# Joining the halves of the exponentials' sums with adding transfers in three pairs, and splitting the PSUM banks of the MLP into two pools

## The chip, the cores and the metric

One NeuronCore of a Trainium2 chip runs the whole program. The metric is the device time of one execution in microseconds. The page and the trace come from one profiled execution of the kernel before, with a span of 915.6 us. In the page PE is TensorE (PEld its weight loads), DVE is VectorE, ACT is ScalarE, POOL is GpSimd and SP is SyncE.

## The reference

Two blocks, one after the other. The first is attention with routing: batch B = 4, H = 8 heads, S = 768 positions, D = 64 columns per head. Queries and keys are each assigned to the nearest of 16 centroids, and a query only sees keys of its own cluster.

```python
mask = q_assign[:, :, :, None] == k_assign[:, :, None, :]
scores = scale * np.matmul(q, k.transpose(0, 1, 3, 2))
scores = np.where(mask, scores, -1000000000.0)
...
attn = np.exp(scores)
attn = attn / (np.sum(attn, axis=-1, keepdims=True) + 1e-09)
return np.matmul(attn, v).astype(np.float32)
```

The heads are laid side by side to rows of 512, and the second block is an MLP with 2048 hidden units and a residual:

```python
xn = (x - mu) / np.sqrt(var + 1e-06) * g_ln
ch = np.maximum(xn @ w_ch1, 0.0) @ w_ch2
return (x + ch).astype(np.float32)
```

All of it is computed in float32. The sum of the exponentials over the keys, the denominator of the softmax, is what the first part of the change touches.

## The kernel before

**Attention.** The work goes by pairs of heads: 16 pairs, numbered n = 0 to 15, four to a batch. A pair has two halves of 384 queries, g = 0 and g = 1; each half is one slot of the main loop. A slot has six steps, one for each block of 128 keys. In a step `scores` (L385) multiplies keys with queries for both heads of the pair and adds the mask by another product, and ScalarE takes the exponential of the result into a tile `e` (L380), with keys on the partitions and the queries of both heads side by side. Two steps share one tile of `e`, so a slot fills three tiles of 128 x 1536. `weigh` (L397) multiplies the values with `e`.

**The sums.** `add_up` (L415 to L438) adds the three tiles of a slot on VectorE into a tile `two`: first two of them (L432), then the third (L435). `two` still holds two halves of 768 columns, for the even and the odd steps. For pairs in `NARROW` (7, 8, 9, 10, 14) one more VectorE addition joins the halves (L437); for the others both stay. `sums` notes which halves there are.

**The denominator.** `finish(n, 0)` (L446 to L465) sums `two` over its 128 partitions by products with a matrix of ones into the PSUM tile `den_ps` (L451): four matmuls for a half, one for each head and each half of the queries, set beside one another on 32 columns of the array each. With both halves that is eight matmuls, with one joined half it is four. ScalarE copies the result to `dsb` (L460), and GpSimd's queue sends it by DRAM to `rdens` in another layout (`flat`, L462, and L463). `finish(n, 1)` takes the reciprocal (L467), sends it back to DRAM (`row`, L469) and loads it broadcast over the partitions (`rb`, two transfers, L477). `finish(n, 2)` and `finish(n, 3)` multiply the weighed values by it and store them.

**The order.** In the attention loop the instructions of TensorE, VectorE, ScalarE and GpSimd are in the order in which the program is written: nothing is moved by a scheduler there. SyncE's queue alone is left to it. In the first slot of pair n the order on TensorE is: the six scores, the denominator of pair n - 1, the centroid similarities of pair n + 1 (`sim_ps`, L304), the six weighings. In GpSimd's queue the first slot has `flat` and `rdens` of pair n - 1 and, at its end, a transfer that adds a converted part of the weights (`w<-tb`, L273, also an adding transfer, in `join_weight`). In the second slot it has `row` and `rb` of pair n - 1. The written order of the end of a slot matters for the change:

```python
            for i in own:
                weigh(i)
            add_up(n, slot, (0,))
            if slot and n and nxt:
                finish(n - 1, 1)
            if nxt:
                add_up(n, slot, (1,))
            if m:
                join_weight(m)
```

**PSUM.** PSUM has eight banks. In attention they are six for the scores, one for `a_ps` and `den_ps`, and one for the rest. After attention `stage.close()` gives them back, and one pool `ps_m` with eight banks is opened for all that follows.

**The MLP.** Per batch, each layer is computed in blocks with seven products for each eight of a plain block product. In both layers three kinds of PSUM tiles occur. `x_ps` and `z_ps` live long: a product is written, read out, and the next product is added into the same bank later. `y_ps` is written once and read once. Besides these, `stat_ps` (L564) and `flag_ps` (L762) are short transposes: the statistics of the rows of the next batch, and in batch 0 a check on the range of the denominators, which VectorE reads at L764. In the second layer (`second_layer`) each part runs over three row tiles `tt`, with eight matmuls (sixteen records) per product. From the second layer of batch 0 on only TensorE's order is as written; the other engines are ordered by the scheduler.

Of the kernel before, what the change touches and what calls it, by code (L numbers as in the profile page):

```python
# [13 lines left out]
ALU = mybir.AluOpType  # L14
AX = mybir.AxisListType
PSUM = bass.MemoryType.PSUM
# [3 lines left out]
def kernel(  # L20
# [11 lines left out]
    nc = tc.nc  # L32
# [3 lines left out]
    P = 128  # L36
# [19 lines left out]
    def pool(name, bufs, **kw):  # L56
        return stage.enter_context(tc.tile_pool(name=name, bufs=bufs, **kw))
# [10 lines left out]
    pools = {"t": pool("ps_t", 1, space=PSUM), "conv": conv}  # L68

    def ps(name, dt=F32, n=512):  # L70
        return pools["t"].tile([P, n], dt, tag="t", name=name)

    pairs = [(b, pr) for b in range(B) for pr in range(NPAIR)]
    loaded = {n: {} for n in range(len(pairs))}
# [1 line left out]
    TWICE = 7  # L76

    NARROW = (7, 8, 9, 10, 14)


    def load_blocks(n, name):
# [112 lines left out]
    def turn_centroids():  # L194
        ct_ps = ps("ct_ps")
        nc.tensor.transpose(ct_ps[:D, : H * NCL], c_sb, ident[: H * NCL, : H * NCL])
        ct_v = ct_ps[:D, : H * NCL].rearrange("p (r j c) -> p r j c", j=2, c=NCL)
        for j in range(2):
            nc.vector.tensor_copy(cT[j * D : (j + 1) * D, :, j, :], ct_v[:, :, j, :])
# [97 lines left out]
    def prep_sims(n):  # L297

        _, pr = pairs[n]
        sim = ps("sim_ps")  # L300
        for side in range(2):
            for g in range(NHALF):
                r = (g * 2 + side) * Q
                nc.tensor.matmul(  # L304
                    sim[r : r + Q, :HC],
                    cT[:, pr, :, :].rearrange("p j c -> p (j c)"),
                    prepared[n][side][:, g * HC : (g + 1) * HC],
                    start=True,
                    stop=True,
                    tile_position=(0, r),  # L310
                )
        prepared[n]["sim"] = sim
# [50 lines left out]
    sums = {}  # L363
# [51 lines left out]
    def add_up(n, g, parts=range(2)):  # L415
        u = (n * NHALF + g) * NT // 2
        if n + 1 == len(pairs):

            es = xpool.tile([P, 2, HC], F32, tag="row", name="es", bufs=2)
            e = [two[:, h] for two in [soft.pop(u + m) for m in range(NT // 2)] for h in range(2)]  # L420
            for m in range(1, NT):
                nc.vector.tensor_tensor(es, e[0] if m == 1 else es, e[m], ALU.add)
            sums[n, g] = [es]
            return
        if 0 in parts:
            if g == 0:
                two = xpool.tile([P, 3, S], F32, tag="sums", name="two", bufs=2)[:, :2]
            else:
                two = last.tile([P, 2, S], F32, tag="two", name="two", bufs=1)
            two = two.rearrange("p h (j c) -> p h j c", j=2)  # L430
            sums[n, g] = two
            nc.vector.tensor_tensor(two, soft.pop(u), soft.pop(u + 1), ALU.add)  # L432
        if 1 in parts:
            two = sums[n, g]
            nc.vector.tensor_tensor(two, two, soft.pop(u + 2), ALU.add)  # L435
            if n in NARROW:
                nc.vector.tensor_tensor(two[:, 0], two[:, 0], two[:, 1], ALU.add)  # L437
            sums[n, g] = [two[:, h] for h in range(1 if n in NARROW else 2)]  # L438

    def finish(n, part):
        b, pr = pairs[n]
        if part == 0:
            den = ps_a.tile([P, 512], F32, tag="a", name="den_ps") if n + 1 < len(pairs) else ps("den_ps")
            parts = len(sums[n, 0])  # L446
            for h in range(parts):
# [238 lines left out]
    with tc.manual_schedule(engines=order | {mybir.EngineType.Pool}):  # L686
        for u in range(len(pairs) * slots):
            n, slot = divmod(u, slots)
# [30 lines left out]
# [7 lines that stand above are left out]
# [42 lines left out]


    stage.close()  # L770
    pools["t"] = pool("ps_m", 8, space=PSUM)
    hid = pool("hid", 2)
    rest = ExitStack()
    pools["conv"] = rest.enter_context(tc.tile_pool(name="rest", bufs=1))
# [443 lines left out]
```

## Time and profile before

| | |
|---|---|
| time, median of 3 | 916.98 us (916.11 to 920.95) |
| span of the profiled execution | 915.6 us |
| attention, up to the last denominator | 0 to about 329.6 us |
| MLP | 329.7 us to the end |
| TensorE busy | 905.1 us |
| VectorE busy | 605.7 us, most of it in attention |
| DMA, mean over the span | 98 GB/s |
| granted TensorE clock | 0.999 |
| `den_ps` matmuls, two halves or one (L451) | 200 records, 19.2 us busy |
| last addition of `two` (L435) | 30, mean 1756 ns |
| joining addition on VectorE (L437) | 10, mean 958 ns |
| adding transfer `w<-tb`, 256 KB | 32, median 6.1 us to landing |

The page has a row for each group of instructions, with its busy time, the mean of one in ns, and the idle time of its engine just before it with what ended that. A float32 matmul leaves two records, so 200 records are 100 matmuls. A DMA row on GpSimd shows the time in which the transfer was issued; its time to landing is given apart. VectorE's load is uneven: in the slices of attention it is busy for seven to nine tenths, in the MLP for three to six.

### The profile page before, as it was taken

How to read it: one execution, taken by the hardware profiler on the slowest of the kernel's cores; microseconds unless marked ns; L12 is line 12 of the kernel's file. 1: busy time of each engine (PE TensorE's matmuls, PEld its weight loads, DVE VectorE, ACT ScalarE, POOL GpSimd, SP SyncE). 2: the span in 40 equal slices, each digit the busy share in tenths (PEclk: the TensorE clock that was granted, in tenths of full speed). 3: DMA queues.
4: the chain of work that ended last, by engine and by line, in shares of the span. 5: the costliest groups of instructions: out<-in, count | busy, mean ns of one | idle time of the engine just before them, and what ended most of it. 6: DMA issues, size and time to landing. Idle time of an engine off the chain costs nothing.

```text
span 915.6 us, 12228 instructions
## 1 busy us (share of the span) xinstructions
PE 905.1 (99%) x4556; PEld 576.9 (63%) x4556; DVE 605.7 (66%) x1060; ACT 365.7 (40%) x619; POOL 77.3 (8%) x141
## 2 busy tenths in 40 slices
PE   8999999999999999999999999999999999999997
PEld 5444444444444455578885568886558887557886
DVE  7999999899889878988843446542436372445330
ACT  4777777998877643330003330003331001332000
POOL 1122222111121112100000000000000000000000
PEclk9999999999999999999999999999999999999999
DMA  7888999997886346663520003120002120000011
GB/s 151 169 177 160 185 180 196 193 217 142 203 172 123 75 123 156 141 172 116 166 74 0 1 0 104 58 74 7 1 1 92 52 70 29 0 1 13 23 47 38
DMA packets 186579, 89.33 MB, mean 98 GB/s; under 512 B 153632, under 2 KB 170128, under 8 KB 186512
## 3 DMA queue, kind: packets, MB, share of 16 engines
q1 hardware_dynamic: 177200, 73.09, 33.6%
q0 software_dynamic: 7712, 14.99, 8.3%
q8 instruction: 38, 0.62, 0.3%
q10 hardware_dynamic: 1600, 0.39, 0.2%
q14 instruction: 29, 0.24, 0.1%
HBM read 62.52 MB, written 17.52 MB: 87 GB/s over the span
## 4 chain that ended last, share of the span: by engine, by line
PE 65%; ACT 0%; DVE 0%; issue 0%
PE x_ps L880 18%; PE x_ps L787 18%; PE z_ps L880 9%; PE z_ps L787 9%; PE y_ps L880 5%; PE y_ps L787 5%; PE s_ps L385 1%; PE a_ps L397 1%; PE den_ps L451 0%; ACT late L460 0%; DVE o_sb L903 0%; PE stat_ps L564 0%; PE flag_ps L762 0%
## 5 line engine op out<-in xcount | busy, mean ns | idle before, releaser
L380 ACT ACTIVATE e<-s_ps 128x768 f32<-128x768 f32 x192 | 151.7, 812 | 9.2 <-PE s_ps L385 4.6
L385 PE MATMUL s_ps<-t,t 64*128 64x384 f32 x768 | 154.9, 483 | 0.0
L397 PE MATMUL a_ps<-e,v_sb 128*64 128x384 f32 x768 | 130.9, 490 | 0.0
L397 PEld LDWEIGHTS a_ps<-e,v_sb 128*64 128x64 f32 x768 | 52.3, 137 | 75.8 <-issue 62.6
L807 DVE TENSOR_TENSOR h<-z_ps,u 128x384 f32<-128x384 f32 x64 | 35.6, 556 | 88.6 <-PE z_ps L787 67.4
L385 PEld LDWEIGHTS s_ps<-t,t 64*128 64x128 f32 x768 | 68.2, 188 | 35.1 <-issue 34.2
L880 PE MATMUL x_ps<-w2t,h 128*128 128x256 f32 x384 | 84.5, 379 | 0.0
L815 ACT ACTIVATE h<-h 128x384 f32<-128x384 f32 x96 | 49.5, 522 | 86.3 <-DVE h L807 86.3
L880 PEld LDWEIGHTS x_ps<-w2t,h 128*128 128x128 f32 x384 | 72.7, 190 | 10.1
L385 PE MATMUL s_ps<-mask,mask 64*128 64x384 bf16 x384 | 63.0, 324 | 1.1 <-ACT e L380 0.7
L432 DVE TENSOR_TENSOR two<-e 128x1536 f32<-128x1536 f32 x30 | 52.6, 1753 | 14.3 <-ACT e L380 14.0
L802 ACT COPY u<-x_ps 128x384 f32<-128x384 f32 x64 | 30.6, 479 | 75.9 <-PE x_ps L787 75.9
L802 ACT COPY p<-x_ps 128x384 f32<-128x384 f32 x32 | 14.9, 467 | 97.5 <-PE x_ps L787 97.5
L435 DVE TENSOR_TENSOR two<-two,e 128x1536 f32<-128x1536 f32 x30 | 52.7, 1756 | 1.7
L891 DVE TENSOR_TENSOR o_sb<-x_ps,xb 128x256 f32<-128x256 f32 x48 | 20.1, 418 | 49.4 <-PE x_ps L880 49.4
L787 PE MATMUL x_ps<-xn,w 128*128 128x384 f32 x128 | 46.6, 487 | 0.6 <-ACT late L460 0.6
L787 PE MATMUL x_ps<-xn,ws 128*128 128x384 f32 x128 | 46.5, 486 | 0.0
L787 PE MATMUL y_ps<-xn,w 128*128 128x384 f32 x128 | 46.5, 486 | 0.0
L787 PE MATMUL z_ps<-xt,ws 128*128 128x384 f32 x128 | 46.5, 486 | 0.0
L787 PE MATMUL x_ps<-xt,ws 128*128 128x384 f32 x128 | 46.5, 486 | 0.0
L787 PE MATMUL x_ps<-xt,w 128*128 128x384 f32 x128 | 46.5, 486 | 0.0
L787 PE MATMUL z_ps<-xn,ws 128*128 128x384 f32 x128 | 46.5, 486 | 0.0
(151 smaller groups left out, 1330.4 us busy)
## 6 DMA issues: line engine op xcount, KB each, us to landing
raw<-in_moe_w_ch_dram SPq DMA_DIRECT2D x32, 512.0 KB, 5.6
w<-tb POOLq DMA_DIRECT2D x32, 256.0 KB, 6.1
v_sb<-in_v_dram SPq DMA_DIRECT2D x32, 192.0 KB, 5.4
xr<-x_d SPq DMA_DIRECT2D x24, 256.0 KB, 3.1
xb<-x_d SPq DMA_DIRECT2D x48, 128.0 KB, 2.1
out_dram<-o_sb SPq DMA_DIRECT2D x48, 128.0 KB, 1.7
q_sb<-in_q_dram SPq DMA_DIRECT2D x62, 96.0 KB, 3.4
k_sb<-in_k_dram SPq DMA_DIRECT2D x62, 96.0 KB, 5.9
```

What stands on the lines that cost most here:

```text
L380: nc.scalar.activation(e, s[:, :, :HC], AF.Exp, scale=SCALE)
L385: nc.tensor.matmul(s[:, j, :HC], of_keys[:, keys], of_queries[:, o : o + HC], start=part == first, stop=part != first, skip_group_check=True,)
L397: nc.tensor.matmul(acc[j * D : (j + 1) * D, :HC], loaded[n]["v"][:, j, c, :], e[:, j, :], start=(c == 0), stop=(c == NT - 1),)
L432: nc.vector.tensor_tensor(two, soft.pop(u), soft.pop(u + 1), ALU.add)
L435: nc.vector.tensor_tensor(two, two, soft.pop(u + 2), ALU.add)
L787: nc.tensor.matmul(bank[:, :HC], lhs[:, c, :], rhs[:, c, :], start=first and c == 0, stop=c == NDH - 1, skip_group_check=True,)
L802: nc.scalar.copy(t, bank[:, :HC])
L807: nc.vector.tensor_tensor(h, bank[:, :HC], other, ALU.add)
L815: nc.scalar.activation(h, h, AF.Relu)
L880: nc.tensor.matmul(bank[:, :MH], hidden[lhs + (c,)][:, tt * P : (tt + 1) * P], rhs[:, c, :], start=first and c == 0, stop=c == NFH - 1, sk ...
L891: nc.vector.tensor_tensor(o, bank[:, :MH], x, ALU.add)
```

## The change

In the pairs 11, 12 and 13 (`CARRIED`) the two halves of `two` are joined as well, but not by VectorE: a transfer issued from GpSimd's queue reads the second half and adds it onto the first. With that `sums` has one half, and the denominator of these pairs needs four matmuls instead of eight. The transfer is issued in `add_up`, in each of the two slots of a pair, and moves 128 x 768 float32, 384 KB.

In the MLP the eight banks are split: `x_ps` and `z_ps` come from a pool of six, all others (`y_ps`, `stat_ps`, `flag_ps`) from a pool of two. It is meant to keep the short-lived tiles from taking turns with the long-lived ones.

```diff
     def ps(name, dt=F32, n=512):
-        return pools["t"].tile([P, n], dt, tag="t", name=name)
+        p = pools["long" if "long" in pools and name in ("x_ps", "z_ps") else "t"]
+        return p.tile([P, n], dt, tag="t", name=name)
...
     NARROW = (7, 8, 9, 10, 14)
+
+    CARRIED = (11, 12, 13)
...
             if n in NARROW:
                 nc.vector.tensor_tensor(two[:, 0], two[:, 0], two[:, 1], ALU.add)
-            sums[n, g] = [two[:, h] for h in range(1 if n in NARROW else 2)]
+            elif n in CARRIED:
+                nc.gpsimd.dma_start(out=two[:, 0], in_=two[:, 1], accum_op=ALU.add)
+            sums[n, g] = [two[:, h] for h in range(1 if n in NARROW + CARRIED else 2)]
...
     stage.close()
-    pools["t"] = pool("ps_m", 8, space=PSUM)
+
+    pools["long"], pools["t"] = pool("ps_m", 6, space=PSUM), pool("ps_n", 2, space=PSUM)
     hid = pool("hid", 2)
```

## Prediction

> **What bounds the kernel now.** I read the busy shares first, then the slices, then the chain of waits, then TensorE, GpSimd and VectorE in order of time around the denominators of pairs 11 to 13.
>
> ```profile
> PE 905.1 (99%) x4556; PEld 576.9 (63%) x4556; DVE 605.7 (66%) x1060; ACT 365.7 (40%) x619; POOL 77.3 (8%) x141
> ...
> PE   8999999999999999999999999999999999999997
> ...
> DMA  7888999997886346663520003120002120000011
> ```
>
> TensorE is busy 905.1 of 915.6 us, in every slice. Between 34 and 310 us it idles 1.3 us in all, from 329.7 us to the end of its last matmul not at all. The chain that ended last has only matmuls of weight. So TensorE's stream is the time: a matmul taken out gives its time back in full, and each time TensorE waits is paid in full. The DMA row shows engines loaded at eight to nine tenths up to about 275 us (slices 1 to 12 of 22.9 us).
>
> TensorE, the narrow denominator of pair 10 (one half) and what follows it:
>
> ```profile
> 233.71 0.85 PE L451 MATMUL den_ps<-two,ones 128*32 128x384 f32 x8
> 234.38 0.83 PE L304 MATMUL sim_ps<-t,cT 128*32 128x384 f32 x8
> ```
>
> and the wide ones of pairs 12 and 13 (that of pair 11 starts at 253.10, its follower at 254.42):
>
> ```profile
> 273.14 1.50 PE L451 MATMUL den_ps<-two,ones 128*32 128x384 f32 x16
> 274.46 0.83 PE L304 MATMUL sim_ps<-t,cT 128*32 128x384 f32 x8
> ...
> 293.19 1.50 PE L451 MATMUL den_ps<-two,ones 128*32 128x384 f32 x16
> ```
>
> A matmul leaves two records, so x16 is eight matmuls. A wide denominator holds the stream for 254.42 - 253.10 = 1.32 us, a narrow one for 234.38 - 233.71 = 0.67 us.
>
> GpSimd's queue (its rows are the issue of transfers, not their landing; the bracket is its wait before):
>
> ```profile
> 240.43 0.57 POOL L463 DMA_DIRECT2D rdens<-flat  x1 [4.44 <-DMA flat<-dsb]
> 240.99 0.93 POOL L273 DMA_DIRECT2D w<-tb  x1
> 245.67 0.56 POOL L469 DMA_DIRECT2D row<-rdens  x1 [3.74 <-DVE rdens L467]
> 252.54 1.05 POOL L477 DMA_DIRECT2D rb<-row  x2 [6.31 <-DMA row<-rdens]
> ...
> 265.71 0.56 POOL L469 DMA_DIRECT2D row<-rdens  x1 [3.91 <-DVE rdens L467]
> 270.03 1.05 POOL L477 DMA_DIRECT2D rb<-row  x2 [3.76 <-issue]
> ...
> 285.75 0.56 POOL L469 DMA_DIRECT2D row<-rdens  x1 [5.16 <-DVE rdens L467]
> 288.74 1.05 POOL L477 DMA_DIRECT2D rb<-row  x2 [2.42 <-DMA row<-rdens]
> ```
>
> See here that in the second half of each pair GpSimd stands at "rb<-row" until the small "row" has come back from DRAM, and gets past it at 253.6, 271.1 and 289.8 us: just about when TensorE starts the denominators (253.1, 273.1, 293.2).
>
> VectorE ends the second half's sum early (pair 11):
>
> ```profile
> 245.34 1.76 DVE L435 TENSOR_TENSOR two<-two,e 128x1536 f32<-128x1536 f32 x1
> ```
>
> **What the Trainium skill says.** "TensorE: Matmul & The Clock Gate", Architectural detail: GpSimd's queue is strictly first in, first out. The trace agrees: nothing is issued between 246.2 and 252.5. The same page, Part 1: after an idle window of about 3.4 us TensorE's clock is halved until it has been busy as long. No TensorE gap here exceeds 1.2 us, so this trace doesn't show it. "DMA: Bandwidth & Descriptors", Anatomy of one DMA: 2.0 us plus bytes over 436,000 per us. "Collectives: The Full Stack", The bandwidth ceiling: an adding transfer reads two sources, twice the read traffic of a copy. From both I estimate 2.0 + 2 x 0.60 = 3.2 us for the existing adding transfer of 256 KB (w<-tb); its fastest landing in the trace is just that:
>
> ```profile
> DMA to landing us min/median/max: 3.2/6.1/8.4
> ```
>
> **The change, part by part.**
>
> 1. Denominator matmuls. Pairs 11, 12, 13 go from eight to four matmuls: 1.32 - 0.67 = 0.65 us each, 1.95 us off TensorE's stream.
>
> 2. Six adding transfers of 384 KB (128 x 768 x 4 bytes, on chip, half "two" onto the other). None is in the trace. Lower bound: by the pages' price 2.0 + 2 x 0.90 = 3.8 us (estimate). Upper: the slowest w<-tb, 8.4 us. Near 253 us the engines are full (a share of 1.05 in 253 to 263) and w<-tb issued at 260.9 landed in 5.7 us, so I take 6.5 there for half more bytes; 5 around 271 and 4.6 around 290, where w<-tb took 3.3 us and the share falls to 0.58 and 0.16.
>
>  The first half's transfer goes out after "rdens", before w<-tb, about 12 us before the denominator: hidden, although it makes w<-tb, and "row" behind it, later. GpSimd's own 0.9 us or so for each is free: it is busy 8%.
>
>  The second half's transfer stands last in the slot, **behind rb<-row**. Its data are there at 247.1, but it can't be issued before 253.6, 271.1, 289.8. TensorE's second denominator matmul needs it, and TensorE takes its instructions in order; behind it stand the next pair's similarities, the six weighings and everything after. Nothing fills the gap.
>  - Pair 11: 253.6 + 6.5 = 260.1, against 253.1: waits 7.0 us. Bounds 253.6 + 3.8 (4.3 us) and 253.6 + 1 for a later "row" + 8.4 (9.9 us).
>  - A gap of 7 us exceeds the page's idle window; at half clock for 3.4 us TensorE loses 1.7 us. Bounds 0 and 1.7; I take 1.7.
>  - Pair 12, on the old clock of the trace: while TensorE stood the DMA engines caught up, so "row" takes between 2.5 us (as in pair 13) and its old 3.7. Transfer issued at 269.9 to 271.1, say 270.3, + 5 = 275.3, against 273.1: 2.2 us. Bounds 0.6 and 4.0.
>  - Pair 13: 289.8 + 4.6 = 294.4, against 293.2: 1.2 us. Bounds 0.4 and 2.1.
>
>  Each wait moves everything after it by the same amount (den, flat, rdens, reciprocal, row hang on one another), so they add: 7.0 + 1.7 + 2.2 + 1.2 = 12.1 us.
>
> 3. PSUM banks: six for x_ps and z_ps, two for the rest. Before, TensorE waits nowhere for a bank in MLP save 0.6 us at its first product, for ScalarE's copy of the last denominator. x_ps now starts in another bank and gains that: -0.6. y_ps in two banks: a third y_ps in a batch needs the first read; a product lasts 10.36 / 3 = 3.45 us, and VectorE has read y0 at 561.45 where y2 starts at 564.3: hidden in batches 1 to 3. In batch 0 flag_ps takes one of the two banks, and VectorE, in its own order, reads it late:
>
> ```profile
> 412.50 10.53 PE L880 MATMUL y_ps<-w,h 128*128 128x256 f32 x48
> ```
>
> ```profile
> 417.51 0.27 DVE L764 TENSOR_REDUCE flag_f<-flag_ps 1x1 f32<-1x128 f32 x1
> ```
>
>  The second y_ps would start at 412.5 + 3.45 = 415.95 and now waits for 417.8: 1.9 us. Bounds 0 (if VectorE gets to it sooner) and 2.2. x_ps and z_ps hold at most six banks at once; nothing else waits.
>
> Sum: -1.95 + 12.1 - 0.6 + 1.9 = +11.4 us: 916.98 + 11.4 = **928.4 us**.
>
> **Rivals.**
> - *The join is hidden.* The second transfer leaves before rb<-row, or lands by the denominator. For: DVE has the data 6 us ahead, and 3.8 us would fit. Against: the queue's order. 917.0 - 1.95 - 0.6 = 914.4 without the flag's wait, 916.3 with it. This ends not slower.
> - *Short waits.* Transfers land as on an idle machine (3.8 us), the clock stays full, flag is free: 4.3 + 0.6 + 0.4 = 5.3, less 2.55: 919.7 us. For: w<-tb does land in 3.3 at 279.7. Against: at 253 us the engines are full.
> - *Longer waits.* The clock is lost in pair 12 too and landings are at their upper bounds: 9.9 + 1.7 + 4.0 + 1.7 + 2.1 - 2.55 + 1.9 = +18.8, 935.7; beyond that if the later w<-tb and "row" feed back through the reciprocals, some 938.
>
> **How the numbers follow.** My forecast 0.77, short waits 0.10, longer waits 0.08, hidden 0.05. Between them the forecast's own bounds run from about 921 to 935 (all lower ends with the flag's wait: 917.0 - 2.55 + 5.3 + 1.9 = 921.6; upper as above). Range 920.5 to 935. Half a per cent is 4.6 us, to 921.6: slower 0.87, same 0.09 (short waits, most of them), faster 0.04.
>
> **What would show it.** The denominator's four matmuls in pair 11 stretched over some 7 us, released by a DMA "two<-two", shorter gaps in 12 and 13; on GpSimd "two<-two" right after rb<-row; "who waits" with PE den_ps <- DMA two as the largest TensorE entry, 8 to 13 us; matmuls after the first gap longer than before if the clock fell; y_ps <- flag_f at about 1.9 us. I'm wrong if den_ps follows the scores without a gap, if "two<-two" stands ahead of "row", or if time goes in MLP rather than around 253 to 300 us.

## The result, and the profile after

The changed kernel takes 932.55 us (median; 929.73 to 933.39) against 917.89 us for the kernel before in the same comparison: ratio 1.0151, 95% interval 1.0114 to 1.0188 (the quotient of the two medians would be 1.0160). The forecast was 928.4 us, in a range of 920.5 to 935. The profiled execution is the shortest of those timed (929.73 us, span 928.0), so the trace shows a little less than the median loss.

The busy shares and the slices of the page after:

```profile
PE 908.4 (98%) x4532; PEld 577.0 (62%) x4532; DVE 605.1 (65%) x1060; ACT 365.8 (39%) x619; POOL 83.2 (9%) x147
...
PE   8999999999979899999999999999999999999997
...
PEclk9999999999979999999999999999999999999999
```

In the slices, PE is TensorE's busy share and PEclk its granted clock. Twenty-four records are gone from TensorE (twelve matmuls), yet its busy time grew by 3.3 us, and the twelfth slice (255 to 278 us) has fallen to 7 in both rows: TensorE stood, and when it went on its clock was lower. The waits of TensorE, once up to 310 us and once from 330 us on (total, times, longest):

```profile
PE den_ps L456 <- DMA two<-two: 8.9, 2, 7.4
```

```profile
PE y_ps L886 <- DVE flag_f L769: 1.8, 1, 1.8
```

Both waits are new, and they are the two that were forecast. TensorE in order of time in pair 11:

```profile
253.13 0.83 PE L456 MATMUL den_ps<-two,ones 128*32 128x384 f32 x2
261.32 0.86 PE L456 MATMUL den_ps<-two,ones 128*32 128x384 f32 x3 [7.35 <-DMA two<-two]
...
261.98 2.12 PE L307 MATMUL sim_ps<-t,cT 128*32 128x384 f32 x7
264.03 5.67 PE L400 MATMUL a_ps<-e,v_sb 128*64 128x384 f32 x24
```

The first of the four denominator matmuls runs on the first half's sum, which is there. The second needs the second half's, and stands 8.2 us from start to start. Behind it the six weighings take 5.6 us (to 269.64) where they took 4.0 before. GpSimd's queue at the same time:

```profile
245.70 0.57 POOL L474 DMA_DIRECT2D row<-rdens  x1 [2.63 <-DVE rdens L472]
253.42 1.08 POOL L482 DMA_DIRECT2D rb<-row  x2 [7.14 <-DMA xT_d<-rb]
254.48 0.94 POOL L442 DMA_DIRECT2D two<-two  x1
```

"two<-two" leaves right behind rb<-row, 1.35 us after TensorE has started the denominator that needs it, and lands 6.7 us after its issue. The bracket at rb<-row shows what GpSimd waited for last: not "row", which had landed at 252.5, but xT_d<-rb, the store that empties the one buffer of rb, which landed at 252.8. TensorE by stretches (us of stretch, busy and count, granted clock, DMA share, GB/s):

```profile
257.00:261.00 4.00, 0.00 (x0) 0.50 1.24 191
261.00:264.00 3.00, 2.68 (x14) 0.50 0.95 129
264.00:267.00 3.00, 3.00 (x13) 0.50 0.75 266
267.00:270.00 3.00, 3.00 (x20) 0.96 0.50 150
```

The clock had fallen to half while TensorE stood, and stayed there until about 267.2, 5.9 us after it had work again.

Added up to the last denominator, this gives the following (starts of matmuls; the kernel before in brackets). Pair 11, denominator to the end of the weighings: 253.13 to 269.64, 16.51 us (253.10 to 259.22, 6.12): +10.4. Pair 12, denominator to weighings: 283.56 to 285.88, 2.32 us (2.10): +0.2. Pair 13: 303.83 to 307.67, 3.84 us (2.09): +1.75. Sum +12.4; the last denominator starts at 340.62 instead of 328.23, also +12.4. In the MLP the first product comes 0.78 us behind it instead of 1.45 (-0.7), and y_ps waits 1.8. That is +13.5 in all; the last matmul starts 13.8 us later than before (922.86 instead of 909.06), as the wait of y_ps is 2.1 us from start to start. The span of the trace grew by only 12.4, because what follows the last matmul is 1.4 us shorter in this execution.

### The profile page after: what moved, and what is told of

It is laid out like the page before. It is cut to its first block, busy times and chain, and to the rows that moved or that the text cites. A ratio compares the mean times of both kernels' runs of the same rounds, so it can differ in the third digit from the quotient of the medians.

```text
span 928.0 us, 12203 instructions
## 1 busy us (share of the span) xinstructions
PE 908.4 (98%) x4532; PEld 577.0 (62%) x4532; DVE 605.1 (65%) x1060; ACT 365.8 (39%) x619; POOL 83.2 (9%) x147
## 4 chain that ended last, share of the span: by engine, by line
PE 63%; DVE 2%; DMA 0%; issue 0%; DVEq 0%
PE x_ps L793 18%; PE x_ps L886 17%; PE z_ps L886 9%; PE z_ps L793 9%; PE y_ps L793 4%; PE y_ps L886 4%; PE s_ps L388 1%; PE a_ps L400 1%; DVE hs L880 0%; DVE h L881 0%; DMA w<-tb 0%; DVE h L882 0%; DVE w2t L870 0%; PE den_ps L456 0%; DVE o_sb L897 0%
```

## Experiments

**1. The split of the banks alone** (e1_split_only).

```diff
-    CARRIED = (11, 12, 13)
+    CARRIED = ()
```

> Only the split of the PSUM banks; no pair is carried, so the six transfers are gone and pairs 11 to 13 have eight denominator matmuls again. Theory (the loss is TensorE waiting for the joining transfers, which leave GpSimd's queue too late): nearly all of the loss is gone; what is left is the wait of y_ps for flag_f in batch 0, 1.8 us, less 0.6 us at the first MLP product: 1.2 us over the kernel before, ratio 1.001 (0.999 to 1.004). Rival (the two-bank pool costs more than that one wait): 3 us or more over the kernel before, with waits of y_ps in several batches.

918.81 us, ratio 1.0018 (1.0011 to 1.0025). The only new TensorE wait in its trace is y_ps for flag_f, 1.7 us. The ratio lies in the theory's range, and the rival's waits in other batches don't exist.

**2. The carried pairs alone** (e2_join_only), the eight banks in one pool again.

```diff
-    pools["long"], pools["t"] = pool("ps_m", 6, space=PSUM), pool("ps_n", 2, space=PSUM)
+    pools["t"] = pool("ps_m", 8, space=PSUM)
```

> Only the carried pairs; PSUM keeps one pool of eight banks. Theory: the loss stays, less 1.2 us: 12 to 14 us over the kernel before, ratio 1.014 to 1.016, with den_ps waiting 7 to 8 us for the transfer in pair 11. Rival (bank split): under 8 us over before.

930.31 us, ratio 1.0143 (1.0128 to 1.0159), as forecast; den_ps waits 9.6 us for "two<-two", the longest 7.8. The two parts add up: 0.0018 + 0.0143 = 0.0161, within the interval of the whole. Nine tenths of the loss belong to the transfers.

**3. The same bytes, but nobody waits** (e4_aside): each transfer adds onto a tile that nobody reads, and the denominators keep eight matmuls.

```diff
+    aside = const.tile([P, S], F32, name="aside")
+    nc.vector.memset(aside, 0.0)
...
-                nc.gpsimd.dma_start(out=two[:, 0], in_=two[:, 1], accum_op=ALU.add)
-            sums[n, g] = [two[:, h] for h in range(1 if n in NARROW + CARRIED else 2)]
+                nc.gpsimd.dma_start(out=aside, in_=two[:, 1].rearrange("p j c -> p (j c)"), accum_op=ALU.add)
+            sums[n, g] = [two[:, h] for h in range(1 if n in NARROW else 2)]
```

> The six transfers are issued at the same places with the same bytes, but each adds the second half onto a tile that nobody reads; sums keeps both halves and the denominators have eight matmuls, so nobody waits for the transfers. Bank split as in the change. Theory (the wait is the loss, not the traffic): as the split alone, 1 to 2 us over the kernel before, no wait of den_ps. Rival (the added traffic of 2.3 MB delays the loads of q, k, v and the weights in a stretch where the DMA engines are full): 5 us or more over the kernel before, with waits of TensorE or VectorE for loads between 240 and 310 us.

918.91 us, ratio 1.0018 (1.0011 to 1.0026), the same as the split without any transfer. The traffic costs nothing that shows in the time, even where the DMA engines are full. What is lost is lost by waiting for the transfers, not by their bytes as such.

**4. Another place in the queue** (e3_join_ahead).

```diff
-    def finish(n, part):
+    def finish(n, part, between=None):
...
+            if between is not None:
+                between()
             for j in range(2):
                 nc.gpsimd.dma_start(
...
+            early = slot and n in CARRIED
             if slot and n and nxt:
-                finish(n - 1, 1)
-            if nxt:
+                finish(n - 1, 1, (lambda: add_up(n, slot, (1,))) if early else None)
+            if nxt and not early:
                 add_up(n, slot, (1,))
```

"row" is issued just ahead of the second place, and the loop there issues the two transfers of rb.

> Everything as in the change, but in pairs 11 to 13 the second half's joining transfer is issued between row and the two rb transfers, not behind them (the same instructions, another order in GpSimd's queue; VectorE's order is unchanged). Theory (order in the queue): the transfer leaves at about 247.1 us instead of 254.5 in pair 11 and 7 us earlier in the others relative to their denominators; with 5 to 7 us to landing it is there at 252 to 254, so TensorE waits at most 1 us in pair 11 and not at all in 12 and 13, no clock is lost, and the 1.95 us of removed matmuls show: 0 to 2 us below the kernel before plus the 1.2 us of the bank split, ratio 0.998 to 1.001. Rival 1 (an adding transfer of 384 KB is simply too slow or takes the other transfers' bandwidth, wherever it stands): TensorE still waits 4 us or more in pair 11 and the ratio stays above 1.006. Rival 2 (rb, now behind it, comes late for the multiplication that needs it): a new wait of VectorE for rb, ratio above 1.004.

920.81 us, ratio 1.0034 (1.0021 to 1.0046). The same transfers, issued one place earlier, cost some 11 us less. But the forecast of at most 1.001 was missed. GpSimd and TensorE in pair 11 of this kernel:

```profile
247.54 0.57 POOL L474 DMA_DIRECT2D row<-rdens  x1 [2.86 <-DVE rdens L472]
249.50 0.84 POOL L442 DMA_DIRECT2D two<-two  x1 [1.39 <-DVE two L438]
254.97 1.09 POOL L484 DMA_DIRECT2D rb<-row  x2 [4.63 <-DMA xT_d<-rb]
```

```profile
254.97 0.83 PE L456 MATMUL den_ps<-two,ones 128*32 128x384 f32 x2
257.12 0.52 PE L456 MATMUL den_ps<-two,ones 128*32 128x384 f32 x3 [1.32 <-DMA two<-two]
```

"two<-two" left 5.5 us ahead of the denominator, but here took 7.5 us to land, so TensorE still stood: 2.15 us from start to start, and the clock held at 1.00 there. Pairs 12 and 13 show no wait. VectorE's multiplication doesn't wait for rb. So rival 1 has a part in it, in pair 11 alone. The rest of the excess isn't found in the changed stretch. In this trace TensorE is 1.1 us late already at the first denominator and another 0.7 by pair 11, in code that no run here changed. And in the MLP the clock fell behind the wait of y_ps for flag_f, which is 1.9 us here (TensorE by stretches, columns as above):

```profile
417.00:419.60 2.60, 0.71 (x4) 1.00 0.01 4
419.70:423.00 3.30, 3.30 (x9) 0.50 0.61 186
423.10:426.00 2.90, 2.90 (x15) 1.00 0.01 3
```

Some 3.4 us at half clock cost another 1.7 us, which is neither a wait for a transfer nor one that the forecast had.

**5. Keep TensorE busy in the gap** (e5_fill).

```diff
+            if n == CARRIED[0]:
+                for _ in range(34):
+                    nc.tensor.matmul(den[:, :P], ident, ident, start=True, stop=True)
             parts = len(sums[n, 0])
```

> The change, with 34 matmuls (ident by ident, 128 columns, into the bank of den_ps, overwritten afterwards) ahead of pair 11's denominator, so that TensorE has work for about 7.4 of the 8.2 us in which it stood. Theory (half clock after the gap): the transfer lands as before at about 261.3 us, but the clock stays at 1.00 behind it, and the 2.9 us that similarities and weighings lose at 0.50 come back: 929.6 us, ratio to the kernel before 1.011 to 1.014 (the change: 1.0151). Rival (those matmuls are slow for another reason, such as the transfers beside them): ratio stays at 1.015, and with the fill a little too long or the loop a little later 1.016.

In the trace the clock does what the theory says:

```profile
254.42 7.86 PE L453 MATMUL den_ps<-ident 128*128 128x128 f32 x68
262.21 1.30 PE L459 MATMUL den_ps<-two,ones 128*32 128x384 f32 x5
...
264.41 4.09 PE L400 MATMUL a_ps<-e,v_sb 128*64 128x384 f32 x24
273.38 4.09 PE L400 MATMUL a_ps<-e,v_sb 128*64 128x384 f32 x24
```

The granted clock stays at 1.00 throughout, and the weighings take their old 4.09 us beside the same transfers. From denominator to weighings plus weighings pair 11 now takes 7.9 us more than before, against 10.4. In the time it is less clear: 930.4 us, ratio 1.0145 (1.0129 to 1.0161), above the forecast and not separable from the change's 1.0151. In this trace TensorE comes to pair 11 1.3 us later than in the change (254.42 against 253.13), in code that is the same in both, and pair 12, which had no more than 0.9 us of waiting in the change, now takes 3.11 us from denominator to weighings instead of 2.32. So the cost of the half clock is shown in the trace of pair 11, not in the time of the whole.

**6. The same order, but starting with pair 12** (e8_late_two).

```diff
-    CARRIED = (11, 12, 13)
+    CARRIED = (12, 13)
```

> The change with pairs 12 and 13 alone carried, in the change's own order (transfer behind rb). In the change pair 12 showed no wait worth naming. Theory A (that was because the DMA engines caught up while TensorE stood in pair 11): without that stand, row and the transfer of pair 12 are slower and TensorE waits 2 to 4 us there, 1 to 2 in pair 13: 917.5 + 1.2 - 1.3 + 3 + 1.5, ratio 1.003 to 1.008. Theory B (pair 12's transfer is in time by its place alone): wait only in pair 13, ratio 1.001 to 1.002.

931.39 us, ratio 1.0157 (1.0136 to 1.0178): one pair less is carried, and nothing is gained. TensorE in pairs 12 and 13:

```profile
273.22 0.83 PE L456 MATMUL den_ps<-two,ones 128*32 128x384 f32 x2
280.13 0.86 PE L456 MATMUL den_ps<-two,ones 128*32 128x384 f32 x3 [6.07 <-DMA two<-two]
...
282.84 5.38 PE L400 MATMUL a_ps<-e,v_sb 128*64 128x384 f32 x24
...
302.07 0.83 PE L456 MATMUL den_ps<-two,ones 128*32 128x384 f32 x2
305.21 0.52 PE L456 MATMUL den_ps<-two,ones 128*32 128x384 f32 x3 [2.31 <-DMA two<-two]
```

Theory B is out. Theory A's direction is right, its 2 to 4 us too small: pair 12 stands 6.9 us from start to start, and the clock falls to half behind it. Here "row" lands 5.1 us after its issue where it took 1.7 in the change; without the stand in pair 11 the DMA engines have not caught up. (In the kernel before, which has no transfer of the first half ahead of it, it took 3.7.) In pair 13 the clock falls once more, behind a wait of 2.3 us.

**7. VectorE joins the halves instead** (e6_vector_join), no transfers.

```diff
-    NARROW = (7, 8, 9, 10, 14)
+    NARROW = (7, 8, 9, 10, 11, 12, 13, 14)
-    CARRIED = (11, 12, 13)
+    CARRIED = ()
```

> No transfers: VectorE joins the halves in pairs 11 to 13 (they go into NARROW), two additions of 0.96 us per pair; bank split as in the change. Theory: VectorE stands idle for about 2 us per pair before its first addition in a slot, so 1.9 us of additions fit, the 1.95 us of matmuls are gained and 1.2 us lost to the bank split: ratio 0.999 (0.997 to 1.001). Rival (VectorE is full in these pairs, and each addition delays the transposes and one-hot work that TensorE's scores of the next pair wait for): new TensorE waits for t or mask, ratio 1.002 or more over before.

917.95 us, ratio 1.0006 (1.0000 to 1.0013). The ratio lies in the forecast range. VectorE had room in pairs 11 to 13, which all show the narrow form. But in pair 14 TensorE, which is earlier now, comes ahead of VectorE's joined sum, and that pair's denominator is stretched by 0.7 us (the kernel before, then this one):

```profile
309.50 0.85 PE L451 MATMUL den_ps<-two,ones 128*32 128x384 f32 x8 [1.16 <-ACT x L412]
```

```profile
308.20 1.59 PE L456 MATMUL den_ps<-two,ones 128*32 128x384 f32 x8 [1.16 <-ACT x L415]
```

So 1.2 of the 1.95 us arrive at the last denominator. The wait for flag_f is 2.4 us here instead of 1.7.

**8. Without either wait** (e7_two_ahead): pairs 12 and 13 alone, the transfer ahead of rb as in experiment 4, and the check moved by one batch.

```diff
-    CARRIED = (11, 12, 13)
+    CARRIED = (12, 13)
...
-            if b == 0:
+            if b == 1:
                 flag = all_in_range()
```

> Pairs 12 and 13 alone are carried, the second half's transfer issued between row and rb, and the check that uses flag_ps moved from batch 0 to batch 1, where VectorE is idle around it. Theory: no wait for a transfer (in the run with the transfer ahead these two pairs had none), no wait for flag_f; 1.3 us of matmuls and 0.6 us at the first MLP product gained: 915.5 us, ratio 0.998 (0.996 to 1.000). Rival (with pair 11 no longer carried the loaded stretch moves its cost to pair 12): a wait of 1 us or more in pair 12, ratio 1.000 or more.

915.86 us, ratio 0.9986 (0.9977 to 0.9995): a little faster than the kernel before, and in the forecast range. Denominators of pairs 12 and 13:

```profile
273.41 1.25 PE L456 MATMUL den_ps<-two,ones 128*32 128x384 f32 x5
...
293.50 0.85 PE L456 MATMUL den_ps<-two,ones 128*32 128x384 f32 x8
```

Pair 13 has the narrow form, 0.67 us to the similarities. Pair 12 shows no bracket, but it came late to its weighings, as its transfer landed at 274.0, behind the start of the denominator: 2.15 us to the weighings (275.56) where a narrow one takes 1.45. So "no wait" was true of pair 13 only, and pair 12 gained nothing over its wide form (2.10 us). In the MLP TensorE waits for nothing.

**9. The bank split with the check in batch 1** (e11_split_flag1), no pair carried.

```diff
-    CARRIED = (11, 12, 13)
+    CARRIED = ()
...
-            if b == 0:
+            if b == 1:
                 flag = all_in_range()
```

> The bank split alone, no pair carried, with the check that uses flag_ps in batch 1. Theory: the 1.8 us wait of y_ps is gone and 0.6 us at the first product stays gained: ratio 0.9993 (0.998 to 1.000), against 1.0018 for the split alone. Rival: the two-bank pool has another cost and the ratio stays above 1.001.

916.9 us, ratio 0.9995 (0.9986 to 1.0003), against 1.0018 with the check in batch 0. So the split has no other cost that shows than that wait, and without it no gain that is clear of the noise either.

**10. VectorE joins, check in batch 1** (e10_vector_flag1): as experiment 7, and

```diff
-            if b == 0:
+            if b == 1:
                 flag = all_in_range()
```

> No transfers; VectorE joins the halves in pairs 11 to 13 (as in e6_vector_join) and the check with flag_ps moves to batch 1. Theory (the wait for flag_f, 2.4 us in that run, is all that kept it from showing its gain): ratio 0.998 (0.997 to 0.999), against 1.0006. Rival (the wait merely moves, to batch 1 or to VectorE's additions): ratio stays at 1.000 or more.

916.03 us, ratio 0.9984 (0.9978 to 0.9991), as forecast. The gain over experiment 7 is 0.0022, about the wait for flag_f. That the wait cost some of the clock too, as in the trace of experiment 4, is likely but not shown: five of the 21 executions of experiment 7 have a mean granted clock of 0.997, and none of the 21 here is below 0.998.

**11. Three pairs ahead of rb, check in batch 1** (e12_three_ahead): as experiment 4, and

```diff
-            if b == 0:
+            if b == 1:
                 flag = all_in_range()
```

> As e3_join_ahead (three pairs, second transfer ahead of rb) but with the check that uses flag_ps in batch 1. Theory: e3's 1.0034 less the 1.9 us wait for flag_f: 1.0013 (1.000 to 1.0025), what is left over the two-pair run (0.9986) being pair 11, where the transfer still lands too late in the full stretch: a wait of 1 to 3 us there. Rival (e3's excess came from elsewhere, with pair 11 at fault for 0.8 us at most): 0.999 or less.

917.6 us, ratio 1.0002 (0.9994 to 1.0010), between the theory's 1.0013 and the rival's 0.999, at the lower end of the theory's range. In pair 11 den_ps waits 1.6 us for its transfer, and the pair takes 3.86 us from denominator to weighings instead of 2.10; what pairs 12 and 13 and the MLP gain makes up for it. That this is less than experiment 4 minus the wait for flag_f fits the 1.7 us of half clock seen in that trace.

**12. VectorE in pair 11, transfers in 12 and 13** (e9_mixed), transfers ahead of rb, check in batch 1: as experiment 8, and

```diff
-    NARROW = (7, 8, 9, 10, 14)
+    NARROW = (7, 8, 9, 10, 11, 14)
```

> Pair 11 joined by VectorE, pairs 12 and 13 by transfers issued between row and rb, check with flag_ps in batch 1, bank split. Theory: 1.95 us of matmuls and 0.6 us at the first MLP product gained, no wait added: 915.0 us, ratio 0.997 (0.9965 to 0.9985), a little under the run with pairs 12 and 13 alone (0.9986). Rival (the transfers or VectorE's addition cost something that the two-pair run hid): 0.999 or more.

915.21 us, ratio 0.9978 (0.9965 to 0.9991): the lowest of all, though its interval overlaps those of experiments 8 and 10. Its trace has one wait of 1.0 us for a transfer, in pair 12, which takes 3.24 us from denominator to weighings instead of 2.10: "no wait added" was not met there.

## Why the prediction was right, and where its sizes were off

- **The mechanism** was right: the second half's transfer queued behind rb<-row (254.48 us against a denominator at 253.13), and TensorE stood in order behind it. Experiment 3 rules out the traffic by itself, experiment 4 shows that the place in the queue is nearly all of it.
- **Denominator matmuls**, -0.65 us a pair: right. A carried pair without a wait (pair 13 in e3_join_ahead) goes from denominator to similarities in 0.67 us.
- **Pair 11**: forecast 7.0 us, measured 8.2. The landing was sized well (6.5 against 6.7); the issue was 0.9 us later, since rb<-row itself got past its wait later. The allowance of 1 us for a later "row" covered this, but by luck: "row" landed only 0.3 us later than before, and GpSimd then waited for xT_d<-rb, which the prediction doesn't name.
- **The half clock**: the first of two terms outside their bounds. Forecast 1.7 us at most, measured 2.9: 1.3 in the denominators and similarities (261.32 to 264.03, against 1.42 us for the same work in pair 13) and 1.6 in the weighings. The Trainium skill, "TensorE: Matmul & The Clock Gate", Part 1, speaks of a window of about 3.4 us of sustained work before the clock returns, and the prediction counted one such window; here it took 5.9 us, and the measurement decides. The same part says that the window runs freely and doesn't start with the work, so up to two of them, 6.8 us, can pass (an estimate from the page's figure), and 5.9 lies within. The kernel before did show the fall, though not the return: its last matmul ends at 909.4 us, and from 913.7 on the granted clock is 0.50. Experiment 5 shows that the slowness was the clock and not the transfers beside it.
- **Pair 12**: forecast 2.2, measured 0.9 (2.32 us, where a narrow denominator and the similarities take 1.45). The idea that the engines catch up during the stand was right, and more so than I allowed: "row" landed in 1.7 us, below my 2.5. Experiment 6 shows the reverse. The 5 us to landing were met (5.1), but not for the reason given: the shares of 0.58 and 0.16 that the prediction names belong to 283 to 293 and 293 to 303 us, and from 273 to 283 the kernel before has 1.01. (The DMA row also has a 7 in the first and the tenth slice, where the prediction reads eight to nine tenths; no term rests on that.)
- **Pair 13**: forecast 1.2, measured 2.4, outside its bounds too (2.1 at most): "row" took 4.0 us to land there, not the 2.5 of before, so the transfer left later. Its own landing, 4.3, was within 0.3 of the forecast.
- **Sum of the stands**: forecast 12.1, measured 8.2 + 2.9 + 0.9 + 2.4 = 14.4. With 0.2 us less in the MLP that makes +13.5 in the trace where +11.4 was forecast. Part of the miss cancelled, which is luck: pair 11, the half clock and pair 13 were forecast 1.2 us too small each, pair 12 1.3 too large.
- **The price of a transfer**: the lower bound of 3.8 us is an estimate. Its factor of two comes from the Trainium skill, "Collectives: The Full Stack", The bandwidth ceiling, which says it of ReduceScatter's adding step and not of a transfer like these. The fastest of the six landed in 4.0 us, so the estimate fits, but no run here tests the factor alone.
- **Banks**: -0.6 and +1.9 forecast, -0.7 and +1.8 in the trace, shown alone in experiments 1 and 9.
- **Rivals**: "hidden" failed on the order of the queue; with the order changed and the check moved, the best median is 915.21 us (experiment 12) against its 914.4. "Short waits" failed on the full engines at 253 us (6.7 us to landing there, not 3.8), on the clock and on flag_f. "Longer waits" (935.7) is nearer to the median of 932.55 than my own 928.4, but its mechanism did not occur: the clock was not lost in pair 12, and no landing came near 8.4 us.

## What to carry to other kernels

Before an addition is moved from a compute engine to a transfer, look at what stands ahead of it in the issuing queue, not only at when its data are ready: here transfers issued 7.4, 1.7 and 4.0 us after their data were ready brought 14.4 us of standing and slow clock against 1.95 us of matmuls removed. Where the engine that sets the time is made to wait, count the lower clock after the wait as well, and don't expect the second such wait to be like the first. When a pool of banks is split, list everything that draws from the smaller part; a once-only tile that is read late can hold it up.

## What the runs showed of the hardware

- TensorE's clock went to 0.50 during a stand of some 7 us and came back only 5.9 us after work resumed. The stretches at half clock ahead of the last matmul lasted 10.2 us in the change and in e2_join_only, 6.8 and 3.4 in e8_late_two, and 3.4 in e3_join_ahead: all about a multiple of 3.4.
- The length of a wait alone didn't settle whether the clock fell. It fell behind 2.3 us in pair 13 of e8_late_two (0.66 granted in 305 to 308 us) and behind 1.9 us at flag_f in e3_join_ahead; it stayed at full behind 3.0 us at 164 us in e12_three_ahead, behind 2.4 us at flag_f in e6_vector_join and behind 1.3 to 1.9 us in other places. A freely running window, as cited above, would give this, but no run here shifts a wait against it.
- An adding transfer of 384 KB on chip landed in 4.0 to 6.7 us in the change, and in up to 8.7 us in e3_join_ahead and 8.8 in e9_mixed.
- 2.3 MB of extra traffic through engines with a mean busy share of 0.6 to 1.1 (e4_aside, 244 to 303 us) cost no measurable time (1.0018 with and without it).
- It stays open where the time goes that TensorE loses in some executions well ahead of the changed stretch: the trace of e12_three_ahead has a 3.0 us wait of s_ps for an exponential at 164 us, those of e3_join_ahead and e5_fill one of 0.5 and 0.7 at the same place, in code that is the same everywhere.
